# Splitting the first casts, moving row picks, and reordering an exp, a softmax piece and bands in a fused dynamic convolution and feed-forward kernel

## The chip, the cores and the metric

The kernel runs on one core of one Trainium2 chip. The metric is the device time of one execution in microseconds (us). Four executions of the kernel before took 732.46 to 733.31 us, with a median of 732.74 us.

## What is computed

The first stage is a dynamic convolution: for each of 8 x 4096 tokens and each of 8 heads, a softmax over 7 generated weights is applied to the current token and its six predecessors in a 24-column group. Its result, 32768 x 192, goes through a feed-forward layer of width 2048 with a squared ReLU.

```python
# attention part: x (8, 4096, 192), weight_gen (8, 4096, 8, 7)
w = np.exp(weight_gen - max over k);  w = w / (sum over k + 1e-9)
x_pad = six zero rows, then x                       # per batch
x_unf = x_pad[:, s + k, :] as (B, S, K=7, H=8, group=24)
out = einsum('bshk,bskhg->bshg', w, x_unf).reshape(B * S, 192)
# feed-forward part: w_in (192, 2048), w_out (2048, 192)
h = maximum(out @ w_in, 0)
return h * h @ w_out                                # float32
```

## The kernel before

**Tiling.** Time is cut into sub-blocks of 512 tokens. Blocks 0 and 1 are one sub-block each, all later blocks two. For each sub-block, x is held as five overlapping tiles of 128 tokens (`x_t`), and the softmax weights of the same rows as `wr_t`. `st_band` (L381) multiplies a tile's weight rows with a banded mask on VectorE and so makes the band matrices `bd`; the convolution is then small matmuls of x tiles against bands on TensorE (`st_conv_first`, L431, for blocks 0 and 1; `st_conv`, L501, later), whose PSUM output `yp` is copied to `y` in SBUF as float16.

**Feed-forward.** `st_unit` (L554) makes one unit, 128 hidden rows for the 1024 tokens of a block, or 256 hidden rows for the 512 tokens of blocks 0 and 1: matmuls into a PSUM tile `h`, a ReLU on ScalarE into `t1` (L578, written t in the profile), and a square on VectorE into `g` (L582), mostly two units at a time. `st_mm2` (L594) is half of a quarter: 256 tokens' output, accumulated over half of the hidden rows. `o_sum` (L622) takes a finished quarter out of PSUM, with a ScalarE copy (L627) and, from block 2 on, a VectorE add (L629). The next quarter writes the same PSUM banks, so that it waits for these two. Quarters run one block behind the units.

**Softmax.** A `Softmax` object covers 1024, 2048 or 4096 tokens. Its exp runs on ScalarE (L238); `total`, `recip` and `scale` run on VectorE (L245, L252, L260) in pieces of rows, and write `v_first` or `v_big`. Batch 0 has four such parts of 1024 tokens, s0 to s3 (batch 1 has three, from number 4 on). When the last piece of a part of this size is done, `move_rows` issues the DMAs that spread the rows over the tiles `wr_t`, alternately from the SP and the POOL queue (L351).

**Start.** For sub-blocks 0 and 1 there is no time for such DMAs. `select_rows` (L359) picks the rows with matmuls against a selection matrix: eight matmuls a tile into a PSUM tile `pr`, which `copy_rows` (L375) copies to `wr_t` on ScalarE. x of sub-block 0 and the first half of W_in come as float32 and are cast on ScalarE (`x_cast`, L333; L708). `next_rows` (L702) is called after each row of the first convolution and picks a tile of sub-block 1.

**PSUM.** Six of the eight banks form a ring of three tiles of two banks (`ps_h`, tag h) that serves h, yp and most picks; the other two banks are the single tiles o0 and o1. An allocation waits until the tile three places before it in the ring has been read.

**Order.** The order on every engine is that of the program text (a manual schedule); each engine takes its instructions in order and waits on semaphores for others. From block 0 on, the order within a block is a string of steps in `plans` (L725): u is a unit, M half of a quarter, C the convolution of the next block with the loads of x after it, E n, S n and L n an exp piece, a softmax piece and the load of part n, and B n the bands of sub-block n (`st_bands`, L641). The words third and fourth block mean plans 2 and 3. Plans of later blocks are made by rule.

Of the kernel before, what the change touches and what calls it, by code (L numbers as in the profile page):

```python
# [9 lines left out]
def kernel(  # L10
# [26 lines left out]
    nc = tc.nc  # L37
    f32 = mybir.dt.float32
    f16 = mybir.dt.float16

    B, S, D = x.shape
# [9 lines left out]
    P = 128  # L51
    TB = 512
    NBB = S // TB
    NSUB = B * NBB
    BLOCKS = [(0, 1), (1, 1)] + [(n, 2) for n in range(2, NSUB, 2)]
    NBLK = len(BLOCKS)
    NFIRST = sum(n == 1 for _, n in BLOCKS)
# [8 lines left out]
    NT = 5  # L66
# [4 lines left out]
    ROW_ORDER = (0, 1, 2, 3, 4)  # L71
# [9 lines left out]
    p_x = ctx.enter_context(tc.tile_pool(name="p_x", bufs=2))  # L81
# [7 lines left out]
    ps_h = ctx.enter_context(tc.tile_pool(name="ps_h", bufs=3, space=bass.MemoryType.PSUM))  # L89
# [4 lines left out]
    NQ = Dff // WQ  # L94
    w_i = const.tile([P, WQ, 2, NQ + NQ // 2], f16, name="w_i")
# [32 lines left out]
    x_st = {}  # L128
# [10 lines left out]
    def cross_w_in(q):  # L139
        for r0, r1 in ((0, RT), (RT, 0)):  # L140
            nc.sync.dma_start(out=w_i[r0 : r0 + RT, q, 1], in_=w_i[r1 : r1 + RT, q, 0])
# [147 lines left out]
    x_t, wr_t, pr_t, bd_t, yp_t, y_t, g_t, gp_t, t1_t, o_t, o_sb_t = ({} for _ in range(11))  # L289
# [12 lines left out]
    def tile_start(j, i):  # L302

        t1 = (j % NBB + 1) * TB
        return TB - P if i == NT - 1 and t1 in ends(j // NBB) else starts[i]
# [24 lines left out]
            j, x_st[j][:, 0 : NT * D].rearrange("p (t d) -> p t d", t=NT), x[j // NBB], D, nc.sync  # L330
        )

    def x_cast(j, copy):  # L333
        x_t[j] = p_x.tile([P, NT, D], f16, name="xt")
        copy(out=x_t[j].rearrange("p t d -> p (t d)"), in_=x_st[j][:, 0 : NT * D])

    def wr_load(j):
        wr_t[j] = p_wr.tile([P, NT, HP, SL * 2], f16, name="wr")
# [20 lines left out]
    def select_rows(j, s, tiles, places):  # L359

        if j not in wr_t:
            wr_t[j] = p_wr.tile([P, NT, HP, SL * 2], f16, name="wr")
        for i, (pool, tag) in zip(tiles, places):
            pr = pool.tile([P, H * SL], f32, name="pr", tag=tag)
            a = max(j % NBB * TB + tile_start(j, i), 0) - s.t0
            for r in range(s.r):
                c = a + FIRST - 1 - r
                nc.tensor.matmul(
                    out=pr, lhsT=sel[:, c : c + P],
                    rhs=s.v[:, HALO + r].rearrange("p g c e -> p (g c e)"),  # L370
                    start=(r == 0), stop=(r == s.r - 1),
                )
            pr_t[(j, i)] = pr

    def copy_rows(j, tiles):  # L375
        for i in tiles:
            nc.scalar.copy(
                out=wr_t[j][:, i].rearrange("p g c -> p (g c)"), in_=pr_t.pop((j, i))
            )

    def st_band(j, tiles):  # L381


        if j not in bd_t:
            bd_t[j] = p_bd.tile([P, H * NT * STEP], f16, name="bd")
        i = tiles[0]
        lo = STEP * i
        shift = 0 if i == 0 and j % NBB == 0 else lo - tile_start(j, i)
        n = min(STEP, P - shift)
        shape = (P, HP * len(tiles), n // SL, 2 * SL)  # L390
        nc.vector.tensor_tensor(  # L391
            out=bd_t[j][:, H * lo : H * (lo + len(tiles) * n)].rearrange(
                "p (g m c) -> p g m c", g=shape[1], c=2 * SL
            ),
            in0=wr_t[j][:, i : tiles[-1] + 1]
            .rearrange("p t g c -> p (t g) c")
            .unsqueeze(2)
            .broadcast_to(shape),
            in1=mask[:, shift : shift + n]
            .rearrange("p (m c) e -> p m (c e)", c=SL)  # L400
            .unsqueeze(1)
            .broadcast_to(shape),
            op=AluOp.mult,
        )
# [26 lines left out]
    def st_conv_first(j, between=None):  # L431

        s = BLOCKS[j][0]
        y = p_y.tile([P, NK, TB], f16, name="y")
        y_t[j] = y
        yp = ps_h.tile([P, 2, TB], f32, name="yp", tag="h")
        places = [(q, 32 * q, 0) for q in range(4)]
        places += [(q, r0 + 32 * (q - 4), 1) for r0 in (0, RT) for q in (4, 5)]
        for i in ROW_ORDER:
            lo, b = bounds[i], bounds[i + 1]  # L440
            hi = lo + (STEP if tile_start(s, i) == starts[i] else b - lo)
            bd = bd_t[s][:, H * lo : H * hi].rearrange("p (g c e) -> p g e c", g=HP, e=2)
            for later in (True, False):
                for q, p0, k in places:
                    _, ha, hb, pre = quads[q]
                    m, h = (32, hb) if later else (pre, ha)
                    nc.tensor.matmul(
                        out=yp[p0 : p0 + m, k, lo:b],
                        lhsT=x_t[s][:, i, 32 * q : 32 * q + m],
                        rhs=bd[:, h // 2, h % 2, 0 : b - lo],  # L450
                        start=True,
                        stop=True,
                        skip_group_check=True,
                        tile_position=(0, p0),
                    )
            if between:
                between(i)
        if j == 0:
            nc.scalar.copy(out=y[:, 0], in_=yp[:, 0])
            nc.vector.tensor_copy(out=y[:, 1], in_=yp[:, 1])  # L460
        else:
            nc.scalar.copy(out=y[:, 0:2], in_=yp)

# [37 lines left out]
    def st_conv(j):  # L501
# [3 lines left out]
        if j < NFIRST:  # L505
            return st_conv_first(j)
# [134 lines left out]
    def st_bands(j):  # L641
        first = int(j % NBB == 0)
        last = NT - int(tile_start(j, NT - 1) != starts[-1])
        for tiles in (range(first), range(first, last), range(last, NT)):
            if tiles:
                st_band(j, tiles)

    with nc.allow_low_precision("fp16 matmul pipeline"), tc.manual_schedule():
# [31 lines left out]
        s0, s1, s2 = parts[:3]  # L680
# [4 lines left out]
        w_st = p_wg.tile([P, (R + HALO) * HK], f32, name="w_st", tag="wg")[:, 0 : NQ + NQ // 2]  # L685
# [6 lines left out]
        s0.total(0, s0.rh)  # L692
        s0.recip(0, s0.rh)
        s0.scale(0, s0.rh, nc.vector)
        x_cast(0, nc.scalar.copy)
        o0, o1, ring = (ps_o, "o0"), (ps_o, "o1"), (ps_h, "h")
        select_rows(0, s0, ROW_ORDER, (o1, ring, ring, ring, o0))
        copy_rows(0, ROW_ORDER)
        for i in ROW_ORDER:
            st_band(0, (i,))  # L700

        def next_rows(i):  # L702
            n = ROW_ORDER.index(i)
            select_rows(1, s0, (i,), ((o1, ring, ring, o0, o1)[n],))
            if n < 2:
                copy_rows(1, (i,))
            if n == 1:
                nc.scalar.copy(out=w_i[:, 0, 0], in_=w_st)  # L708

        st_conv_first(0, next_rows)  # L710
        copy_rows(1, ROW_ORDER[2:])

        nc.gpsimd.tensor_copy(out=gate, in_=w_st[:, 0:1])
        for q in range(4):
# [8 lines left out]
        steady = "MuMuuu" * 3 + "MuuuMCu"  # L723
        steady_spread = "MuMuuu" * 2 + "MuCMuuu" + "MuMuuu"
        plans = {  # L725
            0: "B1 u u u u E1 C S1 u u M u u",
            1: "L3 u u B2 M E2 B3 u M E2 u u S2 S2 u M u C u M",
            2: "L4 u u u E3 M u u u M B4 u u u u M B5 S3 u u u u M u E3 C u",
            3: "L5 L6 S3 u u u M u u u M u M B6 E4 u u u M u M B7 u u u E4 M u M C S4 u",
        }  # L730


# [24 lines left out]
        for n, s in enumerate(parts):  # L757
            k = n - min(m for m, p in enumerate(parts) if p.b == s.b)
# [4 lines left out]
        for n, s in enumerate(parts[4:], 4):  # L763
            b, f = s.b, s.fb
            k = n - min(m for m, p in enumerate(parts) if p.b == b)
# [16 lines left out]
        for j in range(len(plans), NBLK):  # L782
            plan, u = [], 0
# [59 lines left out]
        for j in range(NBLK):  # L843
            if j + 2 < NBLK:
                load_rows(j + 2)
            if j == 1:
                for q in range(WQ):
                    cross_w_in(q)
            u = 0
            for step in plans[j].split():  # L850
                kind, n = step[0], int(step[1:] or 0)
                if kind == "u":
                    st_unit(j, u)
                    u += 1
                elif kind == "M":
                    next(mm2)
                elif kind == "C" and j + 1 < NBLK:
                    st_conv(j + 1)
                    if j == 0:
                        x_load(3)  # L860
                    elif j + 2 < NBLK:
                        for k in range(BLOCKS[j + 2][0], sum(BLOCKS[j + 2])):
                            x_load(k)
                    if j == 5:
                        load_w_spread()
                    elif j == 6:
                        cross_w_spread()
                elif kind == "E":
                    parts[n].exp(*next(parts[n].exps))
                elif kind == "S":  # L870
                    soft(parts[n])
                elif kind == "B":
                    st_bands(n)
                elif kind == "L":
                    parts[n].load(nc.sync)


        j = NBLK - 1
# [44 lines left out]
```

The softmax here doesn't subtract the row's maximum and nothing guards it: scores larger than these inputs give would overflow.

## Time and profile before

| what | us |
|---|---|
| median of four executions | 732.74 |
| the profiled execution | 732.82 |
| its span, first to last instruction | 731.0 |
| TensorE busy in the span | 725.4 |
| VectorE busy | 626.1 |
| ScalarE busy | 613.0 |
| first h matmul starts (block 0) | 13.36 |
| conv of block 2 starts | 31.61 |
| conv of block 3 starts | 51.40 |
| conv of block 4 starts | 73.49 |

A page of the profile describes one execution. PE is TensorE, PEld its weight loads, DVE VectorE, ACT ScalarE, POOL GpSimd, SP the queue of SyncE. A group of instructions is written as line, engine, operation, output<-input and shapes, then the count; times are us from the start of the span. In a timeline the first two numbers are start and length, and the bracket at the end is the engine's idle time before the group and what ended it. In the chain of waits, each row is a start, a length, and the work that the last instruction of the kernel was waiting for then. TensorE's matmuls are pipelined, and their ends are modelled, so their starts say more than their lengths.

### The profile page before, as it was taken

The numbers are of one execution on the slowest core, as the hardware profiler recorded it, in microseconds if no ns is written. First come the engines' busy times: TensorE is split into PE (matmuls) and PEld (weight loads), VectorE is DVE, ScalarE is ACT, GpSimd is POOL, SyncE is SP. The second block draws the span as 40 slices with busy tenths as digits, with TensorE's granted clock in tenths as the row PEclk, the third lists the DMA queues.
The fourth block names the chain that finished last, engine by engine and source line by source line (L and its number), as shares of the span: only waits on it lengthen the run. The fifth ranks groups of instructions, "written<-read, shape, count | busy, mean of one in ns | idle before, by whom it ended". The sixth has DMA issues, their size and how long they took to land.

```text
span 731.0 us, 30985 instructions
## 1 busy us (share of the span) xinstructions
PE 725.4 (99%) x14053; PEld 529.5 (72%) x14053; DVE 626.1 (86%) x834; ACT 613.0 (84%) x731; POOL 99.8 (14%) x145
## 2 busy tenths in 40 slices
PE   8999999999999999999999999999999999999998
PEld 4658788777777777777777777777777777777777
DVE  6998997998898988888988888988889988778753
ACT  5899888888888888888888888888888888888883
POOL 8231223321001100011000010010000110001000
DMA  9554445684445452455442554333544325444012
GB/s 209 110 117 103 82 85 107 140 150 122 93 66 137 87 95 57 85 117 119 73 69 62 130 111 87 56 75 118 103 87 87 56 51 120 65 87 78 30 45 68
DMA packets 125984, 68.30 MB, mean 93 GB/s; under 512 B 85321, under 2 KB 122140, under 8 KB 125340
## 3 DMA queue, kind: packets, MB, share of 16 engines
q0 software_dynamic: 46192, 19.43, 22.5%
q1 hardware_dynamic: 79516, 46.79, 22.4%
q8 instruction: 110, 1.80, 1.0%
q14 instruction: 22, 0.18, 0.1%
q10 hardware_dynamic: 144, 0.10, 0.0%
HBM read 50.18 MB, written 28.70 MB: 108 GB/s over the span
## 4 chain that ended last, share of the span: by engine, by line
PE 94%; DVE 3%; ACT 1%; issue 1%; DMA 0%; SPq 0%; DVEq 0%
PE o L613 45%; PE h L564 42%; PE yp L485 4%; DVE g L582 1%; DVE bd L391 1%; PE yp L519 1%; PE wp L678 1%; ACT t L578 1%; DMA wr<-v_first 0%; DVE v_first L260 0%; DVE rcp L252 0%; DVE ssum L245 0%; SPq L351 0%; ACT w_i L708 0%; PE h L549 0%
## 5 line engine op out<-in xcount | busy, mean ns | idle before, releaser
L578 ACT ACTIVATE t<-h 128x1024 f16<-128x1024 f32 x512 | 496.6, 1026 | 60.6 <-PE h L564 59.1
L613 PEld LDWEIGHTS <-g 64*128 64x128 f16 (+1 forms) x8032 | 344.6, 94 | 55.1 <-issue 2.5
L613 PE MATMUL o<-w_o,g 64*128 64x192 f16 (+1 forms) x8032 | 380.4, 243 | 0.3 <-DVE o_sb L629 0.2
L582 DVE TENSOR_TENSOR g<-t 128x2048 f16<-128x2048 f16 (+1 forms) x287 | 307.4, 1105 | 28.1 <-ACT t L578 27.8
L564 PE MATMUL h<-y,w_p 64*128 64x512 f16 x2400 | 291.7, 376 | 0.0
L564 PEld LDWEIGHTS <-w_p 64*128 64x128 f16 x2400 | 113.9, 94 | 94.8
L391 DVE TENSOR_TENSOR bd<-wr,mask 128x4160 f16<-128x4160 f16 (+3 forms) x89 | 149.4, 1703 | 1.5 <-DMA wr<-v_first 0.8
L629 DVE TENSOR_TENSOR o_sb<-o,o_sb 128x384 f32<-128x384 f32 x123 | 68.4, 556 | 62.5 <-ACT o_sb L627 61.5
L321 POOL DMA_DIRECT2D xt<-in_x_dram x63 | 52.6, 837 | 415.2 <-PE yp L485 362.5
L627 ACT COPY o_sb<-o 128x384 f32<-128x384 f32 x129 | 61.7, 478 | 45.6 <-PE o L613 44.8
L564 PE MATMUL h<-y,w_i 64*128 64x512 f16 x576 | 70.8, 376 | 0.1
L564 PEld LDWEIGHTS <-w_i 64*128 64x128 f16 x576 | 31.2, 94 | 21.4 <-issue 1.4
L485 PEld LDWEIGHTS <-xt 128*32 128x32 f16 x2000 | 24.6, 95 | 10.6 <-issue 10.6
L260 DVE TENSOR_TENSOR v_big<-ex,rcp 128x112 f16<-128x112 f32 (+5 forms) x180 | 29.9, 237 | 2.1 <-DMA vd<-v_big 1.1
L495 DVE CAST y<-yp 128x1024 f16<-128x1024 f32 x25 | 30.4, 1218 | 0.0
L485 PE MATMUL yp<-bd,xt 128*32 128x104 f16 (+1 forms) x2000 | 28.4, 210 | 0.0
L238 ACT ACTIVATE ex<-wg 128x560 f32<-128x560 f32 (+4 forms) x38 | 25.9, 682 | 1.8 <-DMA wg<-in_weight_gen_dram 1.8
L245 DVE TENSOR_REDUCE ssum<-ex 128x80 f32<-128x560 f32 (+4 forms) x38 | 25.3, 666 | 1.3 <-ACT ex L238 1.3
L495 ACT CAST y<-yp 128x1024 f16<-128x1024 f32 x25 | 25.2, 1006 | 0.0
L252 DVE RECIPROCAL rcp<-ssum 128x80 f32<-128x80 f32 (+4 forms) x38 | 22.8, 601 | 1.3
L311 POOL DMA_DIRECT2D xt<-in_x_dram x7 | 3.9, 553 | 123.8 <-PE yp L485 109.4
L351 POOL DMA_DIRECT2D wr<-v_first x24 | 13.0, 559 | 22.4 <-ACT t L578 11.8
(40 smaller groups left out, 116.8 us busy)
## 6 DMA issues: line engine op xcount, KB each, us to landing
out_dram<-o_sb SPq DMA_DIRECT2D x63, 384.0 KB
xt<-in_x_dram POOLq DMA_DIRECT2D x42, 240.0 KB, 4.8
wg<-in_weight_gen_dram SPq DMA_DIRECT2D x4, 1064.0 KB
xt<-in_x_dram POOLq DMA_DIRECT2D x21, 192.0 KB, 4.7
wr<-vd SPq DMA_DIRECT2D x38, 80.0 KB
vd<-v_big SPq DMA_DIRECT2D x5, 512.0 KB
y<-y SPq DMA_DIRECT2D x100, 24.0 KB
wg<-in_weight_gen_dram SPq DMA_DIRECT2D x3, 616.0 KB
```

Of the source, the lines that this page charges most:

```text
L238: nc.scalar.activation(out=self.ex[:, lo:hi].rearrange("p r g k e -> p (r g) k e"), in_=self.wg[:, lo:hi].rearrange("p r (g e) k -> p (r g ...
L260: eng.tensor_tensor(out=bass.AP(tensor=v.tensor, offset=v.offset + lo * H * SL + lo % SL * 2 + g * SL * 2, ap=[list(v.ap[0]), [H * SL + 2, ...
L321: eng.dma_start(out=dst[:, first:last], in_=ap)
L391: nc.vector.tensor_tensor(out=bd_t[j][:, H * lo : H * (lo + len(tiles) * n)].rearrange("p (g m c) -> p g m c", g=shape[1], c=2 * SL), in0= ...
L485: nc.tensor.matmul(out=yp[p0 : p0 + 32, k - k0, a:b], lhsT=x_t[s][:, i, c0 : c0 + 32], rhs=bd[:, head // 2, e, 0 : b - a], start=True, sto ...
L495: copy(out=y[:, k0 : k0 + 2], in_=yp)
L564: nc.tensor.matmul(out=h[:, half], lhsT=w_in_chunk(w, u, slot, half), rhs=y_t[j][r0 : r0 + RT, k], start=(slot == 0), stop=(slot == NK - 1 ...
L578: nc.scalar.activation(out=t1[:, e], in_=h, func=ActF.Relu)
L582: nc.vector.tensor_tensor(out=g[:, a : e + 1], in0=t1[:, a : e + 1], in1=t1[:, a : e + 1], op=AluOp.mult)
L613: nc.tensor.matmul(out=oo[:, cc * Dm : (cc + 1) * Dm], lhsT=g[r0 : r0 + n, cc * P : (cc + 1) * P], rhs=w_o[r0 : r0 + n, fc, :], start=(fc ...
L627: nc.scalar.copy(out=o_sb, in_=o[0][:, c])
L629: nc.vector.tensor_tensor(out=o_sb, in0=o[1][:, c], in1=o_sb, op=AluOp.add)
```

## The change

In the start, the x cast is made in three pieces, the third after two pick copies. The first convolution writes two PSUM tiles of one bank each instead of one of two banks, and its two copies read one each. The picks of the third and fourth tile of sub-block 1 move from between the rows of that convolution to behind it, and that of the fifth to behind the first unit, as the new step P. The cast of the first half of W_in is divided between ScalarE and VectorE. In the third block one exp piece moves behind the convolution of the next block and its copies; in the fourth, a softmax piece moves behind the first half of a quarter, and a set of bands behind an exp and two units. The bands of sub-block 2 are made in two instructions more finely divided than before: its first two tiles, then the next three.

The order on the SP and POOL queues stays as it was. VectorE has two instructions more. ScalarE has two more, both from the x cast.

```diff
--- before.py
+++ after.py
@@ -330,9 +330,13 @@
             j, x_st[j][:, 0 : NT * D].rearrange("p (t d) -> p t d", t=NT), x[j // NBB], D, nc.sync
         )
 
-    def x_cast(j, copy):
-        x_t[j] = p_x.tile([P, NT, D], f16, name="xt")
-        copy(out=x_t[j].rearrange("p t d -> p (t d)"), in_=x_st[j][:, 0 : NT * D])
+    def x_cast(j, copy, lo, hi):
+        if j not in x_t:
+            x_t[j] = p_x.tile([P, NT, D], f16, name="xt")
+        copy(
+            out=x_t[j][:, lo:hi].rearrange("p t d -> p (t d)"),
+            in_=x_st[j][:, lo * D : hi * D],
+        )
 
     def wr_load(j):
         wr_t[j] = p_wr.tile([P, NT, HP, SL * 2], f16, name="wr")
@@ -433,7 +437,11 @@
         s = BLOCKS[j][0]
         y = p_y.tile([P, NK, TB], f16, name="y")
         y_t[j] = y
-        yp = ps_h.tile([P, 2, TB], f32, name="yp", tag="h")
+        if j == 0:
+            yps = [ps_h.tile([P, TB], f32, name="yp", tag="h") for _ in range(2)]
+        else:
+            yp = ps_h.tile([P, 2, TB], f32, name="yp", tag="h")
+            yps = [yp[:, k] for k in (0, 1)]
         places = [(q, 32 * q, 0) for q in range(4)]
         places += [(q, r0 + 32 * (q - 4), 1) for r0 in (0, RT) for q in (4, 5)]
         for i in ROW_ORDER:
@@ -445,7 +453,7 @@
                     _, ha, hb, pre = quads[q]
                     m, h = (32, hb) if later else (pre, ha)
                     nc.tensor.matmul(
-                        out=yp[p0 : p0 + m, k, lo:b],
+                        out=yps[k][p0 : p0 + m, lo:b],
                         lhsT=x_t[s][:, i, 32 * q : 32 * q + m],
                         rhs=bd[:, h // 2, h % 2, 0 : b - lo],
                         start=True,
@@ -456,8 +464,8 @@
             if between:
                 between(i)
         if j == 0:
-            nc.scalar.copy(out=y[:, 0], in_=yp[:, 0])
-            nc.vector.tensor_copy(out=y[:, 1], in_=yp[:, 1])
+            nc.scalar.copy(out=y[:, 0], in_=yps[0])
+            nc.vector.tensor_copy(out=y[:, 1], in_=yps[1])
         else:
             nc.scalar.copy(out=y[:, 0:2], in_=yp)
 
@@ -641,7 +649,8 @@
     def st_bands(j):
         first = int(j % NBB == 0)
         last = NT - int(tile_start(j, NT - 1) != starts[-1])
-        for tiles in (range(first), range(first, last), range(last, NT)):
+        split = 2 if j == BLOCKS[NFIRST][0] else first
+        for tiles in (range(first), range(first, split), range(split, last), range(last, NT)):
             if tiles:
                 st_band(j, tiles)
 
@@ -692,23 +701,29 @@
         s0.total(0, s0.rh)
         s0.recip(0, s0.rh)
         s0.scale(0, s0.rh, nc.vector)
-        x_cast(0, nc.scalar.copy)
+        x_cast(0, nc.scalar.copy, 0, 1)
+        x_cast(0, nc.scalar.copy, 1, 3)
         o0, o1, ring = (ps_o, "o0"), (ps_o, "o1"), (ps_h, "h")
         select_rows(0, s0, ROW_ORDER, (o1, ring, ring, ring, o0))
-        copy_rows(0, ROW_ORDER)
+        copy_rows(0, ROW_ORDER[:2])
+        x_cast(0, nc.scalar.copy, 3, NT)
+        copy_rows(0, ROW_ORDER[2:])
         for i in ROW_ORDER:
             st_band(0, (i,))
 
         def next_rows(i):
             n = ROW_ORDER.index(i)
-            select_rows(1, s0, (i,), ((o1, ring, ring, o0, o1)[n],))
             if n < 2:
+                select_rows(1, s0, (i,), ((o1, ring)[n],))
                 copy_rows(1, (i,))
             if n == 1:
-                nc.scalar.copy(out=w_i[:, 0, 0], in_=w_st)
+                c = (NQ + NQ // 2) // 2
+                nc.scalar.copy(out=w_i[:, 0, 0, 0:c], in_=w_st[:, 0:c])
+                nc.vector.tensor_copy(out=w_i[:, 0, 0, c:], in_=w_st[:, c:])
 
         st_conv_first(0, next_rows)
-        copy_rows(1, ROW_ORDER[2:])
+        select_rows(1, s0, ROW_ORDER[2:4], (o1, o0))
+        copy_rows(1, ROW_ORDER[2:4])
 
         nc.gpsimd.tensor_copy(out=gate, in_=w_st[:, 0:1])
         for q in range(4):
@@ -723,10 +738,10 @@
         steady = "MuMuuu" * 3 + "MuuuMCu"
         steady_spread = "MuMuuu" * 2 + "MuCMuuu" + "MuMuuu"
         plans = {
-            0: "B1 u u u u E1 C S1 u u M u u",
+            0: "u P B1 u u u E1 C S1 u u M u u",
             1: "L3 u u B2 M E2 B3 u M E2 u u S2 S2 u M u C u M",
-            2: "L4 u u u E3 M u u u M B4 u u u u M B5 S3 u u u u M u E3 C u",
-            3: "L5 L6 S3 u u u M u u u M u M B6 E4 u u u M u M B7 u u u E4 M u M C S4 u",
+            2: "L4 u u u E3 M u u u M B4 u u u u M B5 S3 u u u u M u C E3 u",
+            3: "L5 L6 u u u M S3 u u u M u M E4 u u B6 u M u M B7 u u u E4 M u M C S4 u",
         }
 
 
@@ -871,6 +886,9 @@
                     soft(parts[n])
                 elif kind == "B":
                     st_bands(n)
+                elif kind == "P":
+                    select_rows(1, s0, ROW_ORDER[4:], (o1,))
+                    copy_rows(1, ROW_ORDER[4:])
                 elif kind == "L":
                     parts[n].load(nc.sync)
```

## Prediction

> **What bounds the kernel now.** I read the page's busy times first, then the table of stretches, the chain of waits over the first 80 us, and last the single instructions around each wait in it.
>
> ```profile
> PE 725.4 (99%) x14053; PEld 529.5 (72%) x14053; DVE 626.1 (86%) x834; ACT 613.0 (84%) x731; POOL 99.8 (14%) x145
> ```
>
> ```profile
> 9.70:13.40 3.70, 3.32 (x121) 2.57 (x122) 1.96 (x5) 2.59 (x7) 3.70 (x7) 1.00 1.22 227
> 52.90:59.70 6.80, 6.46 (x86) 3.64 (x79) 6.73 (x13) 6.80 (x10) 3.57 (x6) 1.00 0.87 200
> 59.70:75.70 16.00, 16.00 (x371) 13.81 (x372) 14.17 (x15) 13.51 (x18) 1.62 (x4) 1.00 0.25 49
> ```
>
> TensorE is full; after its length, a stretch's second number is TensorE's busy time. From 59.7 us on TensorE is never without work (75.7 to 400 us: 324.17 of 324.30). Everything the change touches lies earlier, so its worth is how much sooner TensorE reaches the matmul at 59.66 us; that then goes to the end one for one. The chain (start, length, what) names the waits:
>
> ```profile
> 11.24 1.48 ACT w_i L708
> ...
> 12.72 0.59 ACT y L459
> 13.31 0.02 issue
> 13.34 0.70 DVE y L460
> 14.04 0.04 issue
> 14.08 0.41 PE h L549 x2
> ...
> 29.76 2.37 DVE bd L391 x2
> 32.13 0.04 issue
> 32.17 1.39 PE yp L519 x85
> ...
> 57.29 0.72 DVE v_first L260 x4
> 58.01 1.13 DVE g L582
> 59.14 0.48 DVE o_sb L629
> 59.62 0.04 issue
> 59.66 1.48 PE o L613 x31
> ```
>
> Three places: the first W_in cast with the two y copies one after the other; the conv of block 2 waiting for bands; a matmul of block 3 waiting for an output sum that stands behind a softmax piece. Between them TensorE's starts are evenly spaced (0.75 us a unit in blocks 0 and 1, 0.65 later, 1.32 a quarter half), ScalarE nearly as full.
>
> **What the Trainium skill says.** "PSUM — Partial Sum Buffer", section "PSUM bank collisions raise a hardware error": two engines must not be on one bank and quadrant at once, reads included, while different banks run clean. The halves of yp are two banks of one tile, yet the VectorE copy starts 0.03 us after ScalarE's ends: the tile is kept in order as a whole. "ScalarE: Activation LUTs", "What ACT_TABLE_LOAD costs": 186 ns + 0.833 ns an element, back-to-back ones overlapping 93 ns; the trace agrees (960 columns 0.99, 1536 columns 1.48). "DMA: Bandwidth & Descriptors", "Anatomy of one DMA": some 2 us fixed; here the row DMAs take 1.9 to 3.3 us at 23 us, 4.0 to 4.8 at 58 us.
>
> **Casts, picks, two tiles (to 14.5 us).** The x cast of 960 columns becomes 192, 384 and 384: 0.35, 0.51, 0.51 by that price. The first two fit ScalarE's idle 1.45 us before the first pick copy at 8.67. The third stands after two pick copies: the next copy moves from 9.13 to 9.52 and ends at 9.73, while its band starts at 10.00 behind the other bands. Cost 0 with 0.27 to spare; beyond that all bands slip. The second PSUM tile also waits for that third copy, 0.1 us into the first conv row: 0.
>
> Without picks between its rows, the conv is held by the last band (ends 11.59): last row at 11.64, not 12.31; its copy may start at 12.06 (last matmul 11.83, plus the 0.23 seen from pick matmul 10.90 to copy 11.13). ScalarE's half of W_in (768 columns) takes 0.83 instead of 1.48: 11.24 to 12.07. So y's first half is there at 12.66 instead of 13.31 and the first h matmul starts at 12.72 instead of 13.36: gain 0.64. The W_in half on VectorE is not in the trace. Upper bound: the 512-column y copy, 0.69, plus 256 more at its slope, 0.96; lower: 0.56, estimated from "VectorE: DVE Perf Modes", "The perf-mode tier table" (fp32 in SBUF doubles, 1227 ns at 2048). Behind it stand y's second half and B1. From 11.50 that half of y ends between 12.75 and 13.05; it is wanted at 13.24 (12.72 + 0.21 + 0.31, the spacing of two full-row matmuls and a change to half rows). Both ends give 0, and the wait of 0.20 at 14.08 goes too (13.36 + 0.52 = 13.88).
>
> Given back: the eight matmuls of the last pick now stand between units 0 and 1. Eight took 0.21 from 12.60, with two changes of row group near 0.1 each and the last one's own time: 0.44. Picks 3 and 4 run from 12.0 to 12.7, while TensorE waits for y anyway. Unit 1 starts at 13.90 instead of 14.30. Net 0.40. Bounds: 0.2 if a copy slips, 0.56 if ScalarE leads (its second activation moves from 15.43 to 14.87, when unit 1 ends). The band pair B1 moves from 13.94 to about 13.15; its last part waits for the last pick copy, near 14.7, and is done before its conv at 16.2.
>
> **Bands of block 2 in two.** VectorE is free at 26.77, but waits for all rows until 27.52:
>
> ```profile
> 27.52 4.60 DVE L391 TENSOR_TENSOR bd<-wr,mask 128x4160 f16<-128x4160 f16 x3 [0.75 <-DMA wr<-v_first]
> ```
>
> The last row landed at 27.50, the first two by about 25.5 (an estimate: issued by 23.46, plus 2 us). From 4160 columns 2.33 and 832 columns 0.59: 0.52 ns a column and 0.16 fixed. The first 1664 take 1.03 in the idle time, the other 2496 take 1.46: end 29.08 instead of 29.85, the next tile's last band 31.35 instead of 32.12. The conv's 120 matmuls took 1.88 from 31.61, against 1.53 at 51.40: 0.35 of waiting for that last band. VectorE's lead of 0.77 covers it: gain 0.35, at least 0.15, no more.
>
> **Exp behind the conv's copies (third block).**
>
> ```profile
> 52.43 0.51 ACT L238 ACTIVATE ex<-wg 128x336 f32<-128x336 f32 x1
> 52.84 1.50 ACT L530 CAST y<-yp 128x1024 f16<-128x1024 f32 x2
> 54.21 3.81 ACT L578 ACTIVATE t<-h 128x1024 f16<-128x1024 f32 x4
> ```
>
> The y copy comes forward only to 52.59 (the conv at 73.49 frees it after 1.19): the exp had filled idle time. Then y 0.89, y 0.48, exp 0.41 in steps: the activation follows at 54.37 instead of 54.21. Two units of block 3 start earlier, but the third needs that activation's PSUM buffer: loss 0.15, between a gain of 0.25 and a loss of 0.2.
>
> **Softmax piece and bands (fourth block).** The piece (56.27 to 58.01) goes behind the output sum. The g before that sum then waits only for its activation: near 57.3 instead of 57.92. The sum ends near 59.15, and the quarter at 59.22 + 0.15 waits no more. Its first matmul stood 0.40 before the rest came: gain 0.40. Next late is the piece itself: 59.06 to 60.8 instead of 58.01, so its row DMAs, ten issues on the SP and POOL queues, start 2.8 later. Nothing else on either queue moves past them. Band B6 therefore goes behind the next g: 65.9 instead of 64.06. It is 2.31 long; one g (1.22) and the sum (0.56) stand behind it, with 0.1 overlaps: the sum ends 69.79. The quarter that needs it is due at 70.05 - 0.25 = 69.8: loss 0.05.
>
> **Sum.** 0.40 + 0.35 - 0.15 + 0.40 - 0.05 = 0.95. The profiled execution took 732.82 (span 731.04), giving 731.87; the median 732.74 is 0.08 lower, so 731.8. About 0.2% (1.47 us) is what a measurement tells from no change, and this is 0.13%.
>
> **Rivals.**
> - ScalarE, not TensorE, paces 14 to 23 us, and the exp's two earlier units pay off. For: ScalarE has no gap there, and TensorE's ends are modelled. Against: TensorE's even starts. 0.56 + 0.35 + 0.25 + 0.40 = 1.56: 731.2.
> - Slower: B6's rows land late. The third POOL issue goes out near 62.2; B6 is free of it up to 65.8, a landing of 3.6 us. At 4.8 it costs 1.2 and cancels the gain: 732.9. At the x loads' 7.4 us it costs 3.8: 735.6. It makes the kernel slower by 0.2% from a landing of about 6.0 us. For: the 4.0 to 4.8 seen. Against: those stood behind x loads that landed until 62.72, now before the issues end; without them 1.9 to 3.3.
> - The splits do nothing: the conv's end stays where it was because the third cast holds the bands. Then only 0.35 + 0.40 - 0.2: 732.2.
>
> **How the numbers follow.** Forecast 0.42 (731.4 to 732.1), ScalarE's lead 0.36, late rows 0.12, no effect in front 0.10. Range 730.9 to 733.0: it takes in the first and third rival and late rows up to cancelling, leaving out some 0.15 with larger gains and losses. Faster by over 0.2%: 0.37 (the first rival and a little of the forecast). Within: 0.52. Slower: 0.11.
>
> **What would show it.** First h matmul near 12.7, the VectorE y copy beside ScalarE's; conv of block 2 in 1.53 without a wait; first two bands before 27; the activation after the moved exp not earlier relative to its conv; no wait on o_sb at the quarter near 58.5; B6 not waiting for a DMA. Wrong if unit 1 is not 0.4 earlier, or if B6 or the sum behind it holds a quarter.

## The result and the profile after

The changed kernel takes 731.87 us (median of 42 runs, 731.33 to 732.62), the kernel before beside it 732.87 (60 runs): a ratio of 0.9986, with a 95% interval of 0.9982 to 0.9991. That is 1.0 us less, 0.65 to 1.3 by the interval. The forecast was 0.95 us less, inside the 0.2% that was called no difference. The interval keeps clear of 1, so that many runs do resolve it. It also leaves out the totals of two of the rivals, 1.56 less (ScalarE paces) and 0.55 less (no effect in front).

The busy times on the page of the changed kernel, and the same three stretches (length, then busy time and count of TensorE, its weight loads, VectorE, ScalarE and GpSimd, then granted clock, DMA share and GB/s):

```profile
PE 725.1 (99%) x14053; PEld 530.6 (73%) x14053; DVE 626.8 (86%) x836; ACT 612.4 (84%) x733; POOL 100.0 (14%) x145
```

```profile
9.70:13.40 3.70, 3.41 (x117) 2.38 (x116) 3.59 (x8) 2.25 (x9) 3.70 (x7) 1.00 1.22 212
52.90:59.70 6.80, 6.51 (x96) 4.33 (x95) 5.78 (x11) 6.80 (x11) 1.86 (x3) 1.00 0.95 210
59.70:75.70 16.00, 16.00 (x375) 12.63 (x372) 14.76 (x18) 13.85 (x18) 3.94 (x7) 1.00 0.22 46
```

TensorE's work is the same to 0.3 us, and the span is 730.1 instead of 731.0. In the first stretch VectorE's busy time rises by 1.63. Only 0.55 of that is the W_in cast that it took over; most of the rest is its y copy and the bands behind it, which come earlier and so fall into the stretch. ScalarE's falls by 0.34: its W_in cast is 0.64 shorter, but more pick copies fall into the stretch. The chain of waits of the changed kernel, with lines numbered by the new text (L455 is the first conv, L557 and L572 are the units, L621 the quarters):

```profile
11.49 0.73 ACT w_i L721
12.23 0.54 ACT y L467
12.76 0.04 issue
12.80 0.92 PE h L557 x4
13.72 0.34 PE pr L372 x8
14.06 2.37 PE h L557 x12
...
31.37 1.51 PE yp L527 x100
...
51.89 1.50 ACT y L538 x2
53.39 0.00 ACT ex L238
53.40 0.30 issue
53.70 1.03 ACT t L586
54.73 0.04 issue
54.77 0.82 PE h L572 x6
...
56.92 1.94 PE h L572 x18
58.86 1.32 PE o L621 x32
```

The VectorE copy of y has left the chain. The moved pick stands in it, between units 0 and 1, as what the start gives back. The bands of block 2 and the output sum are gone; a new entry has come, the activation behind the moved exp. The last row of the first conv before, and the conv's last three rows with both halves of the cast and both y copies after:

```profile
12.31 0.36 PE L447 MATMUL yp<-bd,xt 128*32 128x96 f16 x16
```

```profile
11.17 0.99 PE L455 MATMUL yp<-bd,xt 128*32 128x104 f16 x48
11.39 0.84 ACT L721 CAST w_i<-w_st 128x768 f16<-128x768 f32 x1
11.67 0.55 DVE L722 CAST w_i<-w_st 128x768 f16<-128x768 f32 x1
12.17 0.59 ACT L467 CAST y<-yp 128x512 f16<-128x512 f32 x1
12.23 0.69 DVE L468 CAST y<-yp 128x512 f16<-128x512 f32 x1
```

The quarter that waited, before and after:

```profile
59.22 0.24 PE L613 MATMUL o<-w_o,g 64*128 64x192 f16 x1
59.66 1.48 PE L613 MATMUL o<-w_o,g 64*128 64x192 f16 x31 [0.20 <-DVE o_sb L629]
```

```profile
58.68 1.50 PE L621 MATMUL o<-w_o,g 64*128 64x192 f16 x32
```

To add this up, the clock must be read from the same event. The first pick copy, ScalarE's first copy of picked rows to `wr_t`, starts at 8.67 before and at 8.83 after. The only changed work ahead of it is the x cast, and that does not hold it: before, ScalarE stood idle for 1.45 in front of it, after for 1.06. In the other runs below it lies between 8.59 and 9.16, with either form of the start. So I count from that copy. TensorE's starts, relative to it:

| | before | after | difference |
|---|---|---|---|
| first h matmul | 4.69 | 3.97 | -0.72 |
| first matmul of unit 1 | 5.63 | 5.16 | -0.47 |
| conv of block 2 starts | 22.94 | 22.47 | -0.47 |
| unit after that conv | 24.82 | 23.99 | -0.83 |
| first quarter of block 3 | 47.29 | 46.59 | -0.70 |
| unit after the second quarter (which waited) | 52.24 | 51.17 | -1.07 |
| conv of block 4 | 64.82 | 63.77 | -1.05 |

### The profile page after: what moved, and what is told of

It is laid out like the page before. It is cut to its first block, busy times and chain, and to the rows that moved or that the text cites. A ratio compares the mean times of both kernels' runs of the same rounds, so it can differ in the third digit from the quotient of the medians.

```text
span 730.1 us, 30988 instructions
## 1 busy us (share of the span) xinstructions
PE 725.1 (99%) x14053; PEld 530.6 (73%) x14053; DVE 626.8 (86%) x836; ACT 612.4 (84%) x733; POOL 100.0 (14%) x145
## 4 chain that ended last, share of the span: by engine, by line
PE 99%; ACT 1%; issue 0%; DVE 0%
PE o L621 47%; PE h L572 44%; PE yp L493 4%; PE h L557 2%; PE yp L527 1%; PE wp L687 1%; PE yp L455 0%; ACT y L538 0%; PE pr L372 0%; ACT t L586 0%; ACT wr L381 0%; ACT w_i L721 0%; ACT y L467 0%; ACT xt L336 0%; ACT o_sb L635 0%
## 5 line engine op out<-in xcount | busy, mean ns | idle before, releaser
L621 PEld LDWEIGHTS <-g 64*128 64x128 f16 (+1 forms) x8032 | 345.1, 94 | 54.2 <-issue 2.3
L621 PE MATMUL o<-w_o,g 64*128 64x192 f16 (+1 forms) x8032 | 380.6, 243 | 0.0
L572 PE MATMUL h<-y,w_p 64*128 64x512 f16 x2400 | 291.7, 376 | 0.0
L572 PEld LDWEIGHTS <-w_p 64*128 64x128 f16 x2400 | 113.9, 94 | 94.7
L395 DVE TENSOR_TENSOR bd<-wr,mask 128x4160 f16<-128x4160 f16 (+4 forms) x90 | 149.7, 1686 | 1.2 <-ACT wr L381 0.7
L572 PE MATMUL h<-y,w_i 64*128 64x512 f16 x576 | 71.0, 376 | 0.3 <-ACT t L586 0.3
L572 PEld LDWEIGHTS <-w_i 64*128 64x128 f16 x576 | 32.5, 94 | 20.5 <-issue 1.6
```

What stands on the lines that cost most here:

```text
L395: nc.vector.tensor_tensor(out=bd_t[j][:, H * lo : H * (lo + len(tiles) * n)].rearrange("p (g m c) -> p g m c", g=shape[1], c=2 * SL), in0= ...
L572: nc.tensor.matmul(out=h[:, half], lhsT=w_in_chunk(w, u, slot, half), rhs=y_t[j][r0 : r0 + RT, k], start=(slot == 0), stop=(slot == NK - 1 ...
L621: nc.tensor.matmul(out=oo[:, cc * Dm : (cc + 1) * Dm], lhsT=g[r0 : r0 + n, cc * P : (cc + 1) * P], rhs=w_o[r0 : r0 + n, fc, :], start=(fc ...
```

## The experiments

Times are medians. The kernels were run in three groups of four, each beside executions of the kernel before (medians 732.94, 733.21 and 733.06 us): first the start, the bands, the exp and the fourth block's order alone, then the exp taken back, B6 back, one PSUM tile and the whole cast, last the final four below. The intervals of the ratios reach 0.07 to 0.08% to either side, 0.5 to 0.6 us, as much as most effects here. The parts are therefore told apart in the traces, from the first pick copy, one profiled execution for each kernel. Where the times can resolve a part, they agree: the run without the divided cast took 0.62 us more than the run with B6 early, which stood in the same group, and by the traces its conv of block 4 comes 0.66 later.

**The start alone.** All edits up to the step P, without the bands of sub-block 2 and without the two plan lines; here against the changed kernel:

```diff
-        split = 2 if j == BLOCKS[NFIRST][0] else first
-        for tiles in (range(first), range(first, split), range(split, last), range(last, NT)):
+        for tiles in (range(first), range(first, last), range(last, NT)):
...
(plans 2 and 3 as in the kernel before)
```

> The kernel before with the start's edits alone (casts in pieces, picks moved, two PSUM tiles, W_in cast on two engines, the step P). If TensorE paces what follows, unit 1 starts 0.3 to 0.4 us earlier and the time falls by 0.40 us, or by up to 0.55 because VectorE comes to the bands of block 2 a little earlier than TensorE to their conv. If ScalarE paces, 0.56 us or more with the second activation. If the third cast holds the bands: 0.

Measured: 732.53, ratio 0.9994 (0.9986 to 1.0002). The conv of block 2 starts 22.46 after the first pick copy, as in the full change: 0.48 gained. But then that conv takes longer. VectorE of this kernel:

```profile
27.33 4.60 DVE L395 TENSOR_TENSOR bd<-wr,mask 128x4160 f16<-128x4160 f16 x3 [1.06 <-DMA wr<-v_first]
```

and TensorE, start, length and count:

```profile
31.26 2.11 PE L527 MATMUL yp<-bd,xt 128*32 128x104 f16 x120
33.30 0.93 PE L557 MATMUL h<-y,w_i 64*128 64x512 f16 x4
```

The conv takes 2.04 to the next unit, not 1.88. VectorE is ready earlier, but waits 1.06 instead of 0.75 for the rows, so that the bands come only 0.32 earlier. Of 0.48 gained, 0.32 is left. The expectation had the bands arriving earlier than TensorE; it was the other way. How much is lost differs between executions: in four with the old start the row that these bands wait for landed 18.64 to 18.93 after the first pick copy, in six with the new start 18.49 to 18.68.

**The bands of sub-block 2 alone.** The kernel before with the part on `split` of that diff the other way round.

> The kernel before with the bands of sub-block 2 in two instructions, nothing else. My theory: the conv of block 2 takes 1.53 us instead of 1.88, and all of the 0.35 us goes to the end. Rival: the band's wait for the last row's DMA decides, not VectorE's length, and the conv's end does not move: 0.

Measured: 732.38, ratio 0.9993 (0.9986 to 0.9999). TensorE of this kernel:

```profile
31.62 1.60 PE L519 MATMUL yp<-bd,xt 128*32 128x104 f16 x120
33.16 0.93 PE L549 MATMUL h<-y,w_i 64*128 64x512 f16 x4
```

The conv takes 1.54 instead of 1.88, the whole 0.34 less, and the first unit after block 3's second quarter is 0.35 earlier as well. So in these executions the start gains 0.32 alone, the bands 0.35 alone, and both 0.83 together, 0.16 more than the sum. With the bands in two, the start's gain is not lost again to the wait for rows; the size of that part is as uncertain as the landing of the rows. In the changed kernel:

```profile
26.21 1.02 DVE L395 TENSOR_TENSOR bd<-wr,mask 128x1664 f16<-128x1664 f16 x1
27.47 3.73 DVE L395 TENSOR_TENSOR bd<-wr,mask 128x2496 f16<-128x2496 f16 x3 [0.24 <-DMA wr<-v_first]
```

The first part runs before the last row is there, the second still waits 0.24 for it.

**The exp alone,** in the kernel before.

```diff
-            2: "L4 u u u E3 M u u u M B4 u u u u M B5 S3 u u u u M u E3 C u",
+            2: "L4 u u u E3 M u u u M B4 u u u u M B5 S3 u u u u M u C E3 u",
```

> The kernel before with the exp of the third block behind the conv's copies, nothing else. My theory: slower by 0.15 us, seen in the first quarter of block 3 starting 0.15 us later against the conv before it; the first two units of block 3 start earlier. Rival (ScalarE's order pays off): faster by up to 0.25 us. No effect: 0.

Measured: 732.94, ratio 0.9998 (0.9990 to 1.0006). TensorE of this kernel, from the conv of block 3 on:

```profile
51.56 1.57 PE L519 MATMUL yp<-bd,xt 128*32 128x104 f16 x120
53.06 2.25 PE L564 MATMUL h<-y,w_i 64*128 64x512 f16 x18
55.60 0.82 PE L564 MATMUL h<-y,w_i 64*128 64x512 f16 x6 [0.29 <-ACT t L578]
56.24 1.50 PE L613 MATMUL o<-w_o,g 64*128 64x192 f16 x32
```

From conv to first quarter it is 4.68 instead of 4.56: the third unit waits for the activation behind the exp. That is the expected loss, 0.12. But from conv to the unit after the second quarter it is 9.51 in both kernels: that quarter waits for its output sum anyway, and the 0.12 vanishes in this wait. The loss was right, its way to the end was not: alone, it costs nothing. The size is well founded: in all eight traces of kernels with the exp moved this stretch is 4.68 or 4.69, in the six others 4.55 or 4.56.

**The exp taken back in the changed kernel**, where that wait is gone:

```diff
-            2: "L4 u u u E3 M u u u M B4 u u u u M B5 S3 u u u u M u C E3 u",
+            2: "L4 u u u E3 M u u u M B4 u u u u M B5 S3 u u u u M u E3 C u",
```

> The changed kernel with the exp of the third block back ahead of the conv's copies. My theory: from the conv of block 3 to the first quarter after it 4.56 us as before the change, not 4.69, and since nothing waits for the output sum any more, all of 0.13 us goes to the end: 1.1 us below the kernel before. Rival (the move hides in the same slack that it did alone): no difference from the changed kernel.

Measured: 731.91, ratio 0.9981 (0.9973 to 0.9988). From conv to first quarter 4.55 instead of 4.69, and the unit after the second quarter comes 51.06 after the first pick copy instead of 51.17. So the move costs 0.11 to 0.14 us of the changed kernel. The median's interval overlaps that of the changed kernel.

**The fourth block's order alone,** in the kernel before.

```diff
-            3: "L5 L6 S3 u u u M u u u M u M B6 E4 u u u M u M B7 u u u E4 M u M C S4 u",
+            3: "L5 L6 u u u M S3 u u u M u M E4 u u B6 u M u M B7 u u u E4 M u M C S4 u",
```

> The kernel before with the fourth block's order alone (softmax piece, exp and bands moved). My theory: faster by 0.35 us: 0.40 us of waiting for the output sum gone, at most 0.1 us given back where the bands delay the sum of the third quarter. Rival (rows land late): the bands wait for a DMA and TensorE waits 0.4 us or more near 70 us; no gain or slower.

Measured: 732.54, ratio 0.9994 (0.9985 to 1.0002). From conv 3 to the unit after the second quarter 9.14 instead of 9.51: 0.37 gained, and the conv of block 4 is as much nearer to conv 3, so nothing is given back. Nothing near 70 us waits for a DMA. (Ahead of that, where this program is still that of the kernel before, its conv of block 2 took 2.02 instead of 1.88: VectorE waited 0.87 for the rows, not 0.75.)

**B6 back in its old place** in the changed kernel, to see when its rows land:

```diff
-            3: "L5 L6 u u u M S3 u u u M u M E4 u u B6 u M u M B7 u u u E4 M u M C S4 u",
+            3: "L5 L6 u u u M S3 u u u M u M B6 E4 u u u M u M B7 u u u E4 M u M C S4 u",
```

> The changed kernel with the bands B6 back in their old place, ahead of the exp and the next g, so that they show when the rows land. My theory: the rows land within 3.6 us of their issue, the bands start by 65 us, and TensorE loses 0 to 0.2 us. Rival (rows land late, 4.8 us or more after the issue): the bands start at 66.3 us or later and TensorE waits 1 us or more near 70 us.

Measured: 731.98, ratio 0.9983 (0.9976 to 0.9990). VectorE of this kernel:

```profile
62.61 0.56 DVE L637 TENSOR_TENSOR o_sb<-o,o_sb 128x384 f32<-128x384 f32 x1 [0.33 <-ACT o_sb L635]
63.41 2.32 DVE L395 TENSOR_TENSOR bd<-wr,mask 128x4160 f16<-128x4160 f16 x1 [0.24 <-DMA wr<-v_first]
```

The bands wait 0.24 for the last row and start at 63.41, not 66.3. The POOL queue's row DMAs take 1.9 to 2.5 us in this run, and 1.8 to 2.2 in the changed kernel, where they took 4.0 to 4.8 before. The rival of late rows is refuted. The conv of block 4 comes 0.05 earlier than in the changed kernel: moving B6 gave nothing, and moving S3 alone does as well.

**The first conv in one PSUM tile again**, in the changed kernel:

```diff
-            yps = [ps_h.tile([P, TB], f32, name="yp", tag="h") for _ in range(2)]
+            yp = ps_h.tile([P, 2, TB], f32, name="yp", tag="h")
+            yps = [yp[:, k] for k in (0, 1)]
```

> The changed kernel with the first conv in one PSUM tile of two banks again. My theory: VectorE's copy waits for ScalarE's, ends near 13.5 instead of 12.9, and the half-row matmuls of unit 0 start 0.2 us later; that goes to the end: 0.2 us slower than the changed kernel. Rival (the copies side by side are what the start's gain is): unit 0 ends 0.5 us later or more.

Measured: 732.34, ratio 0.9985 (0.9979 to 0.9992). VectorE's copy waits for ScalarE's, and unit 1 starts 5.41 after the first pick copy instead of 5.16; the conv of block 2 also comes 0.25 later:

```profile
13.16 0.69 DVE L469 CAST y<-yp 128x512 f16<-128x512 f32 x1 [0.46 <-ACT y L468]
```

**The W_in half cast whole on ScalarE**, in the changed kernel:

```diff
-                nc.scalar.copy(out=w_i[:, 0, 0, 0:c], in_=w_st[:, 0:c])
-                nc.vector.tensor_copy(out=w_i[:, 0, 0, c:], in_=w_st[:, c:])
+                nc.scalar.copy(out=w_i[:, 0, 0], in_=w_st)
```

> The changed kernel with the W_in half cast whole on ScalarE. My theory: the first y copy waits for it until about 12.9, the first h matmul starts at 13.5 instead of 12.80, and 0.7 us is lost to the end: this division carries the start's gain. Rival (moving the picks carries it): 0.2 us lost or less.

Measured: 732.60, ratio 0.9990 (0.9984 to 0.9997). ScalarE:

```profile
11.71 1.48 ACT L720 CAST w_i<-w_st 128x1536 f16<-128x1536 f32 x1
13.08 0.59 ACT L467 CAST y<-yp 128x512 f16<-128x512 f32 x1
```

The first h matmul comes 4.57 after the first pick copy, not 3.97, and the conv of block 2 0.59 later. Without the division the start is 0.1 slower than before the change, since the pick between the units stays. So the start needs the division, and it needs two PSUM tiles for 0.25. The parts do not add, since each wait covers others. But the division is not enough by itself. Before, two things held the first y copy until nearly the same time: from the first pick copy, the W_in cast ended at 4.05 and the last matmul of the first conv at 4.00; the copy started at 4.05. Moving the picks out of the conv brought that last matmul to 3.33, and with the division the copy starts just then, at 3.34. With the picks moved and the cast whole it starts at 3.93, 0.12 sooner than before. No run divides the cast and leaves the picks; by these times an estimate of its gain is at most 0.05. It takes both.

**More work on ScalarE**, to see which engine paces 14 to 31 us. In the changed kernel a step X behind unit 1 (units are counted from 0) makes two small copies into an unused tile; the output does not depend on them:

```diff
-            0: "u P B1 u u u E1 C S1 u u M u u",
+            0: "u P B1 u X u u E1 C S1 u u M u u",
...
+                    for _ in range(2):
+                        nc.scalar.copy(out=spare, in_=wr_t[0].rearrange("p t g c -> p (t g c)")[:, 0:64])
```

> The changed kernel with two small ScalarE copies more (64 columns each, into an unused tile) behind unit 1's activation, some 0.25 us together. My theory (TensorE paces from unit 1 on): the conv of block 1 starts where it did and the conv of block 2 at most 0.1 us later. Rival (ScalarE paces that stretch): both, and the end, come 0.2 to 0.25 us later.

Measured: 732.01, ratio 0.9984 (0.9978 to 0.9991), 0.37 more than the changed kernel in the same group. The copies cost more than I expected:

```profile
15.75 0.51 ACT L892 COPY spare<-wr 128x64 f16<-128x64 f16 x2
16.17 1.93 ACT L586 ACTIVATE t<-h 128x1024 f16<-128x1024 f32 x2
```

Unit 3's activation comes 0.43 later, the conv of block 1 at the same 7.52, the conv of block 2 0.25 later. Neither expectation holds. An estimate from these two numbers: ScalarE's delay reaches TensorE only beyond about 0.43 - 0.25 = 0.18 us. TensorE then paces the changed kernel there, but with so little lead that ScalarE is next. The start had moved unit 3's activation by 0.62 and TensorE by 0.47, which accounts for 0.15 of that lead; by the same estimate the two were level within some 0.03 before the change.

**No pick between the units.** This follows from the readings: before its last row the first conv waits 0.28 for a band (11.53 to 11.80), room for most of a pick.

```diff
...
+            if n == 3:
+                select_rows(1, s0, (ROW_ORDER[2],), (o0,))
+                copy_rows(1, (ROW_ORDER[2],), nc.vector.tensor_copy)
...
-        select_rows(1, s0, ROW_ORDER[2:4], (o1, o0))
-        copy_rows(1, ROW_ORDER[2:4])
+        select_rows(1, s0, ROW_ORDER[3:], (o1, o0))
+        copy_rows(1, ROW_ORDER[3:])
...
-            0: "u P B1 u u u E1 C S1 u u M u u",
+            0: "B1 u u u u E1 C S1 u u M u u",
```

> The changed kernel with the third pick back ahead of the conv's last row, where TensorE waits for a band, its copy on VectorE, and the fourth and fifth behind the conv, so that no pick stands between units 0 and 1. My theory: the first h matmul comes 0.15 us later, 0.44 us between the units are gone, unit 1 starts 0.3 us earlier and all of that goes to the end. Rival (ScalarE paces): less, 0.1 to 0.15 us, since the second activation then waits for the first.

Measured: 731.65, ratio 0.9981 (0.9975 to 0.9988). The changed kernel in the same group took 731.64, so the times show no gain over it. In the trace the first h matmul comes 0.21 later, the conv of block 1 0.24 earlier, the conv of block 2 0.19 earlier. Most of the 0.3 is there; 0.05 is lost within the conv of block 1. ScalarE does not explain that by the estimate above: unit 3's activation comes 0.09 earlier, and with a lead of 0.18 TensorE could gain 0.27. The cause is open.

**All three together**: the pick in the gap, the exp and B6 in their old places, as a diff against the run just told of.

```diff
-            2: "... u u u u M u C E3 u",
-            3: "... u u u M u M E4 u u B6 u M u M ...",
+            2: "... u u u u M u E3 C u",
+            3: "... u u u M u M B6 E4 u u u M u M ...",
```

> The same, and with the third block's exp and B6 in their old places. My theory: 0.12 us more from the exp and 0.05 us from B6, together 0.45 us below the changed kernel and 1.4 us below the kernel before. Rival (the two moves do nothing): 0.3 us below the changed kernel.

Measured: 731.54, ratio 0.9977 (0.9970 to 0.9985), the lowest ratio of all, but its interval overlaps that of the changed kernel, which took 731.64 in the same group, so it is not shown to be faster than that. In its trace, from the first pick copy, the conv of block 4 comes 0.22 earlier than in the changed kernel, not 0.45. Between the convs of blocks 1 and 2 this one execution lost 0.16 against the kernel with the pick in the gap, though that stretch of the program is the same. The time goes within the conv of block 1, as the 0.05 did: a weight load of TensorE stands for 0.17 there with nothing waited for that the profile shows. The POOL queue of this execution had stood 0.67 for a W_in load; whether the two are connected is open.

**The changed kernel once more.**

> The changed kernel itself once more, beside the others. Every theory: 0.9 to 1.1 us below the kernel before; from the first pick copy to the conv of block 2 22.47 us again, while the first pick copy itself may come 0.1 to 0.3 us earlier or later with the arrival of the first loads.

Measured: 731.64, ratio 0.9981 (0.9974 to 0.9987), 1.4 us less in that group where 1.0 was measured first. From the first pick copy to the conv of block 2 it is 22.46, to that of block 4 63.76: these two traces repeat to 0.01 us where the time moves by 0.4. That is not so wherever a DMA or an unnamed stop comes in: of the same program text, the conv of block 2 in the run with the fourth block's order alone took 0.14 longer than in the kernel before, and the conv of block 1 in the kernel with all three together took 0.16 longer than in that with no pick between the units.

## Why the prediction was right

By its own steps, the predicted gain and what the traces of the kernel before and the changed one give:

| step | predicted | measured |
|---|---|---|
| first h matmul earlier | 0.64 | 0.72 |
| wait for y's second half gone | 0.20 | 0.20 |
| pick between units 0 and 1 | -0.44 | -0.45 |
| start, sum | 0.40 | 0.47 |
| bands of block 2 | 0.35 | 0.36 |
| exp | -0.15 | -0.13 |
| quarter's wait for the sum | 0.40 | 0.37 |
| bands B6 and the sum behind them | -0.05 | -0.02 |
| sum | 0.95 | 1.05 |

The third row is the time from unit 0's last matmul to unit 1, 0.66 (13.33 to 13.99) against 0.21 before; the second is what is left of the start's sum. The rest are differences of the table of TensorE's starts. The steps say more than the total: the range of the prediction, 730.9 to 733.0, took in no change as well, and the difference of the medians is known to 0.3 us only.

- **The start.** The mechanism was as predicted. The cast and the end of the first conv were both to release the y copy near 12.06, and both holds did go. By the times given with the whole cast above, neither edit alone would have brought this gain.
- **The unknown cast.** The estimate from the Trainium skill, "VectorE: DVE Perf Modes", "The perf-mode tier table", was 0.56 for 768 columns in SBUF; the trace shows 0.55. It agrees, and the upper bound of 0.96 was not needed. The copies of y now run side by side, at 12.17 and 12.23.
- **The first h matmul** came 0.08 sooner than predicted, since ScalarE's y copy starts as the conv's last matmul ends, 0.06 before its W_in cast does.
- **The third cast** hides as said: with it, the first conv starts 1.06 after the first pick copy in both kernels.
- **The split bands** gave the predicted time for a reason that was partly missed. They do not only end the old wait; they also keep the start's gain from a wait that it would have met. The start and the bands measured singly add up to 0.16 less. One sum of this step was off by 0.1, without consequence: 2496 columns at 1.46 us instead of 4160 at 2.33 give VectorE a lead of 0.87, not 0.77, and the traces show 0.87 (4.60 to 3.73).
- **The exp** cost what was predicted, but only because the quarter's wait for the sum was taken away in the same change; the prediction did not say that the cost would vanish without that.
- **The rivals.** Late rows: refuted by the run with B6 early. No effect in front: refuted, the conv of block 2 starts 0.47 earlier. ScalarE's lead: not in force in the changed kernel, but by the estimate above only 0.18 us away, which the even starts of TensorE did not show.
- **"TensorE is never without work" after 59.7 us** was too strong. The numbers beside it, 324.17 of 324.30, left 0.13 out. In several executions a quarter near 99.6 us stops in front of its 26th matmul, for different lengths:

```profile
98.18 1.07 PE o L613 x25
99.25 0.46 issue
99.70 0.50 PE o L613 x7
```

This is the chain of the run with the fourth block's order alone. The kernel before stops there for just that 0.13, the one with the exp alone for 0.47, the one with the split bands alone not at all. No engine or buffer is waited for that the profile shows. It is part of what makes spans differ by more than the parts do.

## What to carry to other kernels

Where one engine is full, look for the few waits in it, and price each edit by the start of that engine's next instruction, not by the busy time moved. A saving that is taken in front of a second wait is partly lost there, and a loss can vanish in one. Two things can hold the same instruction until nearly the same time, as the cast and the conv did here: then remove both, and test parts both alone and in the whole. Compare traces from an event that the change does not touch. Here stretches in which engines wait only for each other repeated to about 0.02 us, so that differences of 0.1 could be read, where medians of a dozen runs could not tell 0.5. Stretches that hang on the landing of a DMA, or in which an engine stops without a named wait, differed by 0.15 and more in the same program: for those, look at more than one trace.

## What the runs showed of the hardware

- Row DMAs of the POOL queue took 4.0 to 4.8 us in the kernel before, where the x loads issued ahead of them on that queue were still landing until 62.72 us, and 1.8 to 2.2 in the changed kernel, issued 2 us later, with the last x load landing at 61.52. In the four traces with the fourth block's old order the first of them was issued 3.6 to 4.7 us before the last x load landed, and came 0.31 to 0.41 us behind that landing.
- Two copies of 64 columns on ScalarE delayed the next activation by 0.42 us and the one after it by 0.43, though a pick copy of the same width between two activations delayed it by 0.28 at most (14.68 to 14.96).
- TensorE stopped within a quarter, at the same matmul in different kernels, for 0 to 0.47 us, with nothing waited for that the profile shows.
